# Trace order and conversion pacing in a fused attention and two-layer expert kernel: next gates and first steps before outputs

## The chip, the core and the metric

The kernel runs on one core of a Trainium2 chip. The metric is device time in microseconds for one execution. The core has a matmul engine (TensorE, PE in the rows), a vector engine (VectorE, DVE), a scalar engine (ScalarE, ACT), a general engine (GpSimd, POOL) and a queue engine for transfers (SyncE, SP). Each follows its own list of instructions in order and waits where an input is not there.

## The reference

Windowed attention with four sink columns feeds two dense layers. Shapes: batch 2, 8 heads, 768 tokens, head width 64, so 1536 tokens of 512 channels. All in float32.

```python
x = attn_out.transpose(0, 2, 1, 3).reshape(1536, 512)
g = x @ w_gate                       # 512 x 1536
x = (g / (1 + exp(-g)) * (x @ w_val)) @ w_out      # layer 1, w_out 1536 x 512
h = x @ w_in                         # layer 2, 512 x 2048
out = (max(h, 0) + alpha * min(h, 0)) @ w_out2     # 2048 x 512
```

The weights arrive as 64-bit floats.

## The kernel before

Each product is made of three passes on split operands: high part times high part, low times high, high times low. Weights are split by a conversion, hidden values by `split_hidden` (L691): `hh` on ACT (L692), then `hl` on DVE (L693).

The 1536 tokens are three passes (b = 0, 1, 2) of 512. Layer 1 has a first chunk of four weight columns of 128 (`Moe1.unit`), then four units of two columns (`Duo1.unit`, c = 0 to 3). Units 0 and 3 are plain (`Duo1.plain`, L971): per pass two gate projections (12 matmuls of 512 columns each), two value projections, four outputs of 6 matmuls. Units 1 and 2, and units 1 to 7 of layer 2 (`Duo2.unit`, L1069; unit 0 is plain), treat passes 0 and 1 with a Strassen chain (`Chain.step`, L880): nine steps in `ORDER7`, seven of them products of 6 matmuls into PSUM tiles `pa`, `pb`, `pc`, two full projections of pass 2. Between them ACT copies `pa` to `u1` or `u2` (`keep`, L854), and the next product into `pa` waits for that copy. Twelve outputs follow the chain.

Strassen needs sums. Sums of activations are DVE subtractions and splits, a list `later` of which one is taken per traced step: 14 for layer 1 (`Duo1.sums`, L926), 7 for layer 2 (`Duo2.sums`, L1034), the latter after pass 1 of the last plain unit has its result (`put_y`, L1150). Sums of weights are two items (SUMS, kinds 2 and 3) after each pair of weights that a chain uses; POOL makes them (L567 to L570) and casts them to a high half (L573).

`Stream` feeds the weights. A conversion goes through three calls: `start` (L536, ACT takes the magnitude, L549), `bits` (DVE L584, L587, L590 assemble float32, then ACT's high half `wh`, L593; for sums POOL as above) and `low` (L596, POOL's low half `wl`, L599). `step` (L602) runs each where it can, once per traced step (`tick`, L610). The scratch `w_m` of `start` has two buffers, so a `start` waits until the low half or the sums two items back have read theirs. Converted weights lie in 10 slots (12 at times), given back by `done`.

Trace order is priority: a planner lays out each engine's list before the run, taking of the instructions that are ready by its own times the one traced first. `g.soon()` raises the hidden values. Within `fast` (L1135) `run` (L1219) goes through the units after attention, unit by unit; `verdict` (L363) checks input ranges once the last weight is converted, and ends in a transpose on TensorE and a flag.

Of the kernel before, what the change touches and what calls it, by code (L numbers as in the profile page):

```python
# [11 lines left out]
AF = mybir.ActivationFunctionType  # L12
# [27 lines left out]
VB = 6  # L40
LAG = 2
SOON = 400
ORDER = ((0, 3), (1, 2), (4, 5))
EARLY = 4
WARM = 9
# [317 lines left out]
def verdict(nc, g):  # L363
    scratch = g.t_p.tile([P, T], F32, tag="hid", name="scratch")
    ok, okw = scratch[:, 0:B * H * NQ], scratch[:, B * H * NQ:B * H * NQ + NW]
    nc.vector.tensor_scalar(out=ok, in0=g.nb, scalar1=9.0e8, scalar2=None, op0=ALU.is_lt)
    red = g.red
    nc.vector.tensor_scalar(out=okw, in0=g.wsum, scalar1=WLIM, scalar2=None, op0=ALU.is_lt)
    nc.vector.tensor_reduce(out=red[:, 4:5], in_=okw, axis=AX.X, op=ALU.min)
    nc.vector.tensor_reduce(out=red[:, 0:1], in_=ok, axis=AX.X, op=ALU.min)  # L370
    one = g.const.tile([P, 1], F32, name="one")
    nc.vector.tensor_reduce(out=one, in_=red, axis=AX.X, op=ALU.min)
    ps = g.ps_t.tile([P, 512], F32, tag="ps", name="ps_flag")
    nc.tensor.transpose(ps[:1, :P], one, g.ident)
    fl = g.const.tile([1, 2], F32, name="flag_f")
    nc.vector.tensor_reduce(out=fl[:, 0:1], in_=ps[:1, :P], axis=AX.X, op=ALU.min)
    nc.vector.tensor_scalar(out=fl[:, 1:2], in0=fl[:, 0:1], scalar1=-1.0, scalar2=1.0, op0=ALU.mult, op1=ALU.add)
    g.flag = g.const.tile([1, 1], I32, name="flag")
    nc.vector.tensor_copy(g.flag, fl[:, 1:2])
# [122 lines left out]
class Stream:  # L502
    def __init__(self, nc, g, seq):
        self.nc, self.g, self.seq = nc, g, seq
        self.n_load = self.n_start = self.n_conv = self.n_done = 0
        self.begun = self.halves = None
        self.idle_pool = False
        self.raw, self.w, self.home, self.full = {}, {}, {}, {}
        self.own = range(0)

    def homes(self):

# [39 lines left out]
    def bits(self):  # L552
        nc, g = self.nc, self.g
        (i, rv, m), self.begun = self.begun, None
        kind, src, f, scale, slot = self.seq[i]
        home = self.homes()[0]
        home[1] -= 1
        self.home[i] = home
        wh = home[0].tile([P, KD * P], F32R, tag="wh", name="wh")
        wl = home[0].tile([P, KD * P], F32R, tag="wl", name="wl")  # L560
        self.n_conv += 1
        if kind > 1:
            h = KD * P // 2
            a = self.full[i - kind]
            if kind == 2:
                b, m = self.full[i - 1], self.spare[:, 0:KD * P]
                nc.gpsimd.tensor_tensor(out=m[:, 0:h], in0=b[:, 0:h], in1=b[:, h:], op=ALU.add)  # L567
                nc.gpsimd.tensor_tensor(out=m[:, h:], in0=m[:, 0:h], in1=a[:, 0:h], op=ALU.subtract)
                nc.gpsimd.tensor_tensor(out=a[:, 0:h], in0=a[:, 0:h], in1=b[:, 0:h], op=ALU.subtract)
                nc.gpsimd.tensor_tensor(out=a[:, h:], in0=a[:, h:], in1=m[:, h:], op=ALU.subtract)  # L570
            else:
                m = a
            nc.gpsimd.tensor_copy(wh, m)  # L573
            self.halves = (i, m, wh, wl)
            return
        self.full[i], self.spare = m, rv.rearrange("p c t -> p (c t)").bitcast(F32)
        lo, hi = rv[:, :, 0], rv[:, :, 1]
        mi, mu = m.bitcast(I32), m.bitcast(U32)
        if slot is None or g.exact:
            nc.vector.tensor_scalar(out=m, in0=m, scalar1=WMAX, scalar2=-WMAX, op0=ALU.min, op1=ALU.max)  # L580
            sign, wi = mi, hi
        else:
            sign, wi = hi, mi
        nc.vector.tensor_scalar(  # L584
            out=wi, in0=mi, scalar1=3, scalar2=0x7FFFFFF8, op0=ALU.logical_shift_left, op1=ALU.bitwise_and
        )
        nc.vector.scalar_tensor_tensor(  # L587
            out=mi, in0=sign, scalar=-(2**31), in1=wi, op0=ALU.bitwise_and, op1=ALU.bitwise_or
        )
        nc.vector.scalar_tensor_tensor(  # L590
            out=mu, in0=lo.bitcast(U32), scalar=29, in1=mu, op0=ALU.logical_shift_right, op1=ALU.bitwise_or
        )
        nc.scalar.activation(wh, m, AF.Copy)  # L593
        self.halves = (i, m, wh, wl)
# [5 lines left out]
        self.w[i] = (wh, wl)  # L600

    def step(self):  # L602
        if self.halves:
            self.low()
        if self.begun and self.room():
            self.bits()
        if not self.begun and self.n_load > self.n_start:
            self.start()

    def tick(self, ahead=RB):  # L610
# [85 lines left out]
class Moe1:  # L696
# [4 lines left out]
    def unit(self, c, b):  # L701
# [10 lines left out]
        for x in range(0, CHUNK, 2):  # L712
            pair = hidden_pair(g)
            pss, sgs = [], []
            for r in range(2):
                ps = g.ps_m.tile([P, 512], F32, tag="ps", name="pg")
                proj(nc, ps, st.get(item(0, x + r)), xh, xl)
                pss.append(ps)
                if r == 0:
                    yield  # L720
            for ps in pss:
                sg = g.t_p.tile([P, T], F32, tag="sg", name="sg")
                nc.scalar.activation(sg, ps, AF.Silu)
                sgs.append(sg)
            yield
            for r in range(2):
                hh, hl = (t[:, r] for t in pair)
                ps = g.ps_m.tile([P, 512], F32, tag="ps", name="pv")
                proj(nc, ps, st.get(item(1, x + r)), xh, xl)
                hid = g.t_p.tile([P, T], F32, tag="hid", name="hid")  # L730
                nc.vector.tensor_tensor(out=hid, in0=ps, in1=sgs[r], op=ALU.mult)
                split_hidden(nc, hid, hh, hl)
                hid_of.append((hh, hl))
                if last and r == 1:
                    st.done(4)
                yield
        if c == 0:
            self.accs[b] = new_acc(g, "acc1")
        acc, home = self.accs[b]
# [181 lines left out]
class Duo1(Duo):  # L921
# [48 lines left out]

    def plain(self, w, last):  # L971

        pairs = {}
        _, gate, _, value = self.sinks(pairs)
        for b in range(NPASS):
            pairs[b] = hidden_pair(self.g)
            for i, sink in ((0, gate), (DUO, value)):
                for r in range(DUO):
                    ps = self.new("ph")
                    proj(self.nc, ps, self.st.get(w + i + r), *self.xs[b])  # L980
                    sink(b, r, ps, False)
                    if b == NPASS - 1 and r:
                        self.st.done(DUO)
                    yield
            y = [big(self.g, n) for n in ("yh", "yl")] if last else None
            for m in range(KD):
                self.output(b, m, w + 2 * DUO, *pairs[b], y)
                yield
            if last:
                self.accs[b][1][1] += 1  # L990
                self.put(y, self.accs[b][0])
        self.st.done(DUO)

    def unit(self, c):
# [7 lines left out]
        for i, room, sink in ((0, room_g, gate), (2 * DUO, room_v, value)):  # L1002
            chain = self.chain(w + i, self.ops, self.xs[2], room, sink)
            yield from chain.steps(ORDER7)
            chain.done()
        for b in (2, 0, 1):
            for m in range(KD):
                self.output(b, m, w + 4 * DUO, *pairs[b])
# [19 lines left out]
class Duo2(Duo):  # L1028
# [40 lines left out]
    def unit(self, c, ys):  # L1069
# [9 lines left out]
        else:  # L1079
# [8 lines left out]
                    self.last()  # L1088
            st.done(DUO)
            w += DUO  # L1090
        for b in (2, 0, 1) if c else range(NPASS):
            yield from self.outputs(c, b, w, *pairs[b])
        st.done(DUO)
# [41 lines left out]
def fast(nc, tc, ctx, g, lim, alpha, qk, vp, vs, w_gate, w_val, w_out, x2_in, x2_out, out):  # L1135
# [77 lines left out]
    add_pool(nc, tc, ctx, g.acc_ps, "acc_p2", 1)  # L1213
    for nm, bufs in (("x_p2", 6), ("u_p", 1), ("h_p2", 1), ("t_p2", 4)):
        setattr(g, nm, ctx.enter_context(tc.tile_pool(name=nm, bufs=bufs)))
    st.idle_pool = True
    asked = False

    def run(units):  # L1219
        nonlocal asked  # L1220
        for u in units:
            for _ in u:
                if later:
                    later.pop(0)()
                st.tick()
                if not asked and st.n_conv == len(st.seq):
                    verdict(nc, g)
                    asked = True

    later.extend(d1.sums())  # L1230
    run([m1.unit(0, 2)])
    assert g.w_ps.pop()[1] == WA
    early.close()
    last = (NF1 - CHUNK) // DUO - 1
    with ExitStack() as inner:
        g.x_p3 = inner.enter_context(tc.tile_pool(name="x_p3", bufs=2, side="right"))
        run([d1.unit(c) for c in range(last)])
        assert not later
    add_pool(nc, tc, ctx, g.w_ps, "w_p3", WA, "right")
    st.own = range(base - 3 * DUO, len(st.seq))  # L1240
    run([d1.unit(last)] + [d2.unit(c, ys) for c in range(NF2 // DUO)])
    assert asked and not later


def general(nc, tc, g, q, k, v, w_gate, w_val, w_out, x2_in, x2_out, out):
# [95 lines left out]
```

## Time and profile before

| | |
|---|---|
| median of three runs | 673.70 us (673.52 to 673.95) |
| profiled execution | 673.82 us |
| its span, first to last instruction | 672.1 us |
| TensorE busy | 645.8 us (96%) |
| VectorE busy | 473.8 us (71%) |
| ScalarE busy | 308.7 us (46%) |
| GpSimd busy | 243.5 us (36%) |
| mean granted TensorE clock | 0.985 |

Times of rows are from the span's start. A group row gives busy time, mean duration, then the idle time of the engine before its instructions and what ended it. A wait row gives total, times and longest.

### The profile page before, as it was taken

The numbers are of one execution on the slowest core, as the hardware profiler recorded it, in microseconds if no ns is written. First come the engines' busy times: TensorE is split into PE (matmuls) and PEld (weight loads), VectorE is DVE, ScalarE is ACT, GpSimd is POOL, SyncE is SP. The second block draws the span as 40 slices with busy tenths as digits, with TensorE's granted clock in tenths as the row PEclk, the third lists the DMA queues.
The fourth block names the chain that finished last, engine by engine and source line by source line (L and its number), as shares of the span: only waits on it lengthen the run. The fifth ranks groups of instructions, "written<-read, shape, count | busy, mean of one in ns | idle before, by whom it ended". The sixth has DMA issues, their size and how long they took to land.

```text
span 672.1 us, 8796 instructions
## 1 busy us (share of the span) xinstructions
PE 645.8 (96%) x3032; PEld 506.1 (75%) x3032; DVE 473.8 (71%) x933; ACT 308.7 (46%) x716; POOL 243.5 (36%) x281
## 2 busy tenths in 40 slices
PE   7789899999999899999999989999999999999996
PEld 3457566767788788888878877888888888887885
DVE  6997877353399636678688579848796969686554
ACT  4767856765265214433643335654434252523040
POOL 3547554334113614571334032425344243430000
PEclk8979899999999999999999998999999999999998
DMA  9854444100004203103232111122121213100005
GB/s 273 261 154 144 147 148 134 32 13 1 1 0 130 91 1 93 64 33 126 94 125 95 33 31 62 55 72 63 63 63 63 88 38 95 32 1 0 1 1 192
DMA packets 37205, 52.30 MB, mean 78 GB/s; under 512 B 4385, under 2 KB 28961, under 8 KB 37153
## 3 DMA queue, kind: packets, MB, share of 16 engines
q1 hardware_dynamic: 34944, 51.65, 24.2%
q8 instruction: 26, 0.43, 0.3%
q10 hardware_dynamic: 2208, 0.01, 0.2%
q14 instruction: 27, 0.21, 0.1%
HBM read 48.51 MB, written 3.15 MB: 77 GB/s over the span
## 4 chain that ended last, share of the span: by engine, by line
PE 86%; DVE 5%; ACT 4%; POOL 2%; issue 1%; DMA 1%; SPq 0%; POOLq 0%; ACTq 0%
PE pa L847 9%; PE pf L1105 7%; PE pf L1107 7%; PE pf L1106 7%; PE ph L679 6%; PE ph L680 6%; PE ph L681 6%; PE pb L847 4%; PE po L1018 3%; PE po L1019 3%; PE po L1020 3%; PE xp L321 3%; PE ps_s L225 2%; PE pc L847 2%; PE po L748 2%; PE pg L679 2%
## 5 line engine op out<-in xcount | busy, mean ns | idle before, releaser
L599 POOL TENSOR_TENSOR wl<-w_m,wh 128x512 fp32r<-128x512 f32 x79 | 110.6, 1405 | 197.5 <-ACT wh L593 176.5
L692 ACT ACTIVATE hh<-hid 128x512 fp32r<-128x512 f32 x84 | 52.8, 631 | 83.4 <-DVE hid L966 37.5
L593 ACT ACTIVATE wh<-w_m 128x512 fp32r<-128x512 f32 x68 | 42.9, 631 | 99.3 <-PE pf L1107 40.7
L693 DVE TENSOR_TENSOR hl<-hid,hh 128x512 fp32r<-128x512 f32 x84 | 72.0, 864 | 19.3 <-ACT hh L692 19.2
L1105 PE MATMUL pf<-wh,hh 128*128 128x512 f32 x192 | 75.3, 392 | 0.0
L1106 PE MATMUL pf<-wl,hh 128*128 128x512 f32 x192 | 75.2, 392 | 0.0
L1107 PE MATMUL pf<-wh,hl 128*128 128x512 f32 x192 | 64.7, 392 | 0.0
L584 DVE TENSOR_SCALAR w_m<-w_m 128x512 int32<-128x512 int32 x68 | 35.2, 517 | 37.8 <-ACT w_m L549 37.8
L1112 DVE TENSOR_TENSOR acc<-pf,acc 128x512 f32<-128x512 f32 x84 | 53.3, 683 | 9.8 <-PE pf L1107 9.6
L549 ACT ACTIVATE w_m<-w_raw 128x512 f32<-128x512 f32 x68 | 45.6, 670 | 22.3 <-POOL wl L599 16.6
L587 DVE SCALAR_TENSOR_TENSOR w_m<-w_raw,w_m 128x512 int32<-128x512 int32 x68 | 52.9, 778 | 1.2
L590 DVE SCALAR_TENSOR_TENSOR w_m<-w_raw,w_m 128x512 uint32<-128x512 uint32 x68 | 50.7, 745 | 1.1
L680 PE MATMUL ph<-xl,wh 128*128 128x512 f32 x128 | 49.8, 389 | 0.0
L681 PE MATMUL ph<-xh,wl 128*128 128x512 f32 x128 | 49.8, 389 | 0.0
L679 PE MATMUL ph<-xh,wh 128*128 128x512 f32 x128 | 49.8, 389 | 0.0
L235 ACT ACTIVATE pr<-ps_s,nb 128x160 f32<-128x160 f32 (+2 forms) x96 | 38.0, 406 | 19.5 <-DVE nb L231 17.0
L225 PE MATMUL ps_s<-th 64*128 64x288 f32 (+2 forms) x192 | 39.2, 443 | 7.7 <-ACT pr L235 6.5
L1107 PEld LDWEIGHTS pf<-wh,hl 128*128 128x128 f32 x192 | 36.0, 188 | 8.1
L1018 PE MATMUL po<-hh,wh 128*128 128x512 f32 x96 | 37.8, 394 | 4.5 <-ACT hh L692 4.5
L1106 PEld LDWEIGHTS pf<-wl,hh 128*128 128x128 f32 x192 | 36.0, 188 | 8.1
L1105 PEld LDWEIGHTS pf<-wh,hh 128*128 128x128 f32 x192 | 36.0, 188 | 8.0
L1023 DVE TENSOR_TENSOR acc<-po,acc 128x512 f32<-128x512 f32 x48 | 30.2, 684 | 13.0 <-PE po L1020 13.0
(212 smaller groups left out, 1517.2 us busy)
## 6 DMA issues: line engine op xcount, KB each, us to landing
w_raw<-in_moe_w_out SPq DMA_DIRECT2D x28, 512.0 KB, 3.3
w_raw<-in_moe_w_in SPq DMA_DIRECT2D x16, 512.0 KB, 3.7
w_raw<-in_moe_w_gate SPq DMA_DIRECT2D x12, 512.0 KB, 4.4
w_raw<-in_moe_w_val SPq DMA_DIRECT2D x12, 512.0 KB, 3.6
th<-in_qk SPq DMA_DIRECT2D x16, 336.0 KB, 3.3
vr<-in_v SPq DMA_DIRECT2D x16, 192.0 KB, 2.7
out<-acc SPq DMA_DIRECT2D x12, 256.0 KB, 2.4
th<-in_qk SPq DMA_DIRECT2D x8, 256.0 KB, 5.3
```

The source lines that it names most:

```text
L587: nc.vector.scalar_tensor_tensor(out=mi, in0=sign, scalar=-(2**31), in1=wi, op0=ALU.bitwise_and, op1=ALU.bitwise_or)
L599: eng.tensor_tensor(out=wl, in0=m, in1=wh, op=ALU.subtract)
L679: nc.tensor.matmul(ps, wh[:, c], chan(xh, kk), start=(kk == 0), stop=False)
L680: nc.tensor.matmul(ps, wh[:, c], chan(xl, kk), start=False, stop=False)
L681: nc.tensor.matmul(ps, wl[:, c], chan(xh, kk), start=False, stop=(kk == KD - 1))
L693: nc.vector.tensor_tensor(out=hl, in0=hid, in1=hh, op=ALU.subtract)
L847: self.nc.tensor.matmul(ps, a[:, c], m[:, k], start=(start and k == 0 and y == 0), stop=(k == 1 and y == 2), skip_group_check=True)
L1018: nc.tensor.matmul(ps, wh[:, mc], hh[:, x], start=(x == 0), stop=False)
L1105: nc.tensor.matmul(ps, hh[:, x, ts], wh, start=(x == 0), stop=False)
L1106: nc.tensor.matmul(ps, hh[:, x, ts], wl, start=False, stop=False)
L1107: nc.tensor.matmul(ps, hl[:, x, ts], wh, start=False, stop=(x == DUO - 1))
L1112: nc.vector.tensor_tensor(out=av, in0=ps, in1=av, op=ALU.add)
```

## The change

After `Moe1`'s last pass and in every unit of the two layers, the generator yields a mark, OUT, before its last outputs. The loop in `fast` stops a unit there, traces the first step of the next unit, then the held outputs, then the rest of the next unit. In plain units the gates of pass b + 1 are traced before the outputs of pass b. `Stream.step` does not begin a conversion in a step in which it issued a low half, once `spaced` is set (after attention). The high half of weight sums is an ACT copy in place of a POOL cast. The 14 sums of layer 1 come every second step. The flag's transpose is split from `verdict` into `decide` and traced in the eighth step after the last conversion (LATE).

```diff
+OUT = "outputs"
+LATE = 8
@@ verdict
     nc.vector.tensor_reduce(out=one, in_=red, axis=AX.X, op=ALU.min)
+    g.one = one
+
+
+def decide(nc, g):
     ps = g.ps_t.tile([P, 512], F32, tag="ps", name="ps_flag")
-    nc.tensor.transpose(ps[:1, :P], one, g.ident)
+    nc.tensor.transpose(ps[:1, :P], g.one, g.ident)
@@ Stream.bits
-            nc.gpsimd.tensor_copy(wh, m)
+            nc.scalar.activation(wh, m, AF.Copy)
             self.halves = (i, m, wh, wl)
@@ Stream.step
+        waits = self.spaced and self.halves
         if self.halves:
             self.low()
         if self.begun and self.room():
             self.bits()
-        if not self.begun and self.n_load > self.n_start:
+        if not waits and not self.begun and self.n_load > self.n_start:
             self.start()
@@ Moe1.unit
+        if last:
+            yield OUT
         if c == 0:
             self.accs[b] = new_acc(g, "acc1")
@@ Duo1.plain
-        for b in range(NPASS):
-            pairs[b] = hidden_pair(self.g)
-            for i, sink in ((0, gate), (DUO, value)):
-                for r in range(DUO):
-                    ps = self.new("ph")
-                    proj(self.nc, ps, self.st.get(w + i + r), *self.xs[b])
-                    sink(b, r, ps, False)
-                    if b == NPASS - 1 and r:
-                        self.st.done(DUO)
-                    yield
+        def first(b, i, sink):
+            if i:
+                pairs[b] = hidden_pair(self.g)
+            for r in range(DUO):
+                ps = self.new("ph")
+                proj(self.nc, ps, self.st.get(w + i + r), *self.xs[b])
+                sink(b, r, ps, False)
+                if b == NPASS - 1 and r:
+                    self.st.done(DUO)
+                yield
+
+        def second(b):
             y = [big(self.g, n) for n in ("yh", "yl")] if last else None
             for m in range(KD):
                 self.output(b, m, w + 2 * DUO, *pairs[b], y)
...
+        yield from first(0, 0, gate)
+        for b in range(NPASS):
+            if b < NPASS - 1:
+                yield from first(b, DUO, value)
+                yield from first(b + 1, 0, gate)
+                yield from second(b)
+        yield from first(b, DUO, value)
+        yield OUT
+        yield from second(b)
         self.st.done(DUO)
@@ Duo1.unit, Duo2.unit: before the outputs
+        yield OUT
@@ fast
-    st.idle_pool = True
+    st.idle_pool = st.spaced = True
+    asked = 0
+    def step():
...
+        if later:
+            x = later.pop(0)
+            if x:
+                x()
+        st.tick()
+        if st.n_conv == len(st.seq):
+            asked += 1
+            if asked == 1:
+                verdict(nc, g)
+            elif asked == LATE:
+                decide(nc, g)
...
-    later.extend(d1.sums())
+    later.extend(x for y in d1.sums() for x in (None, y))
...
+    for u, then in units + [(d2.unit(c, ys), None) for c in range(NF2 // DUO)]:
+        for x in u:
+            if x is OUT:
+                break
+            step()
+            if held:
+                for _ in held[0]:
+                    step()
+                if held[1]:
+                    held[1]()
+                held = None
+        held = u, then
+    for _ in u:
+        step()
```

## Rows read from the trace of the kernel before

**Rows 1.** The page's first section: busy us, share of the span, instructions

```profile
PE 645.8 (96%) x3032; PEld 506.1 (75%) x3032; DVE 473.8 (71%) x933; ACT 308.7 (46%) x716; POOL 243.5 (36%) x281
```

**Rows 2.** Stretches: length, busy PE, PEld, DVE, ACT, POOL, granted clock, DMA share, GB/s

```profile
180.00:672.10 492.10, 480.45 (x2098) 393.62 (x2096) 358.52 (x522) 195.78 (x366) 160.80 (x144) 0.99 0.19 62
226.00:230.00 4.00, 4.00 (x18) 3.31 (x19) 3.80 (x4) 0.13 (x1) 2.08 (x2) 1.00 0.10 19
...
405.45:408.85 3.40, 3.40 (x10) 2.59 (x8) 3.40 (x6) 1.71 (x3) 0.00 (x0) 0.51 0.00 0
...
390.00:430.00 40.00, 37.46 (x158) 30.36 (x157) 36.47 (x48) 22.63 (x39) 14.22 (x12) 0.96 0.12 40
```

**Rows 3.** TensorE's waits from 180 us on: total us, times, longest

```profile
PE po L1018 <- ACT hh L692: 4.5, 2, 2.5
PE pa L847 <- ACT u L857: 1.1, 2, 0.7
```

**Rows 4.** Timeline of TensorE: start, duration, instruction, idle before it and its releaser

```profile
226.00 0.50 PE L1018 MATMUL po<-hh,wh 128*128 128x512 f32 x1 [1.99 <-ACT hh L692]
...
403.99 0.50 PE L1018 MATMUL po<-hh,wh 128*128 128x512 f32 x1 [2.54 <-ACT hh L692]
...
665.73 0.39 PE L1107 MATMUL pf<-wh,hl 128*128 128x512 f32 x1
```

**Rows 5.** Timeline of TensorE, first and last of nine starts at the lower clock

```profile
405.48 0.58 PE L1018 MATMUL po<-hh,wh 128*128 128x512 f32 x1
...
408.85 0.44 PE L679 MATMUL ph<-yh,wh 128*128 128x512 f32 x1
```

**Rows 6.** Timeline of TensorE at full clock, first and fifteenth start, between two Strassen steps

```profile
452.04 0.39 PE L680 MATMUL ph<-yl,wh 128*128 128x512 f32 x1
...
455.22 0.39 PE L847 MATMUL pa<-yh,wh 128*128 128x512 f32 x1
```

**Rows 7.** Chain of waits before 226 us: start, duration, engine, tile, line

```profile
222.41 0.74 POOL w_m L569
...
223.18 0.76 ACT w_m L549 x2
...
223.97 0.04 DVE w_m L584
...
224.60 0.69 DVE hid L966
```

**Rows 8.** Chain of waits before 404 us

```profile
393.86 1.13 DVE acc L833
...
399.84 2.23 DVE acc L833
...
402.68 0.61 DVE hid L966
```

**Rows 9.** Timeline: POOL's first low half for layer 1's units; first output matmul

```profile
189.16 1.29 POOL L599 TENSOR_TENSOR wl<-w_m,wh 128x512 fp32r<-128x512 f32 x1 [15.35 <-ACT wh L593]
...
202.09 0.39 PE L748 MATMUL po<-hh,wh 128*128 128x512 f32 x1
```

**Rows 10.** ACT's waits for POOL from 180 us on: total us, times, longest

```profile
ACT w_m L549 <- POOL wl L599: 14.0, 18, 1.4
...
ACT w_m L549 <- POOL w_m L569: 5.3, 3, 3.0
```

**Rows 11.** Groups from 180 us on: busy us, mean ns, idle before and releasers

```profile
L593 ACT ACTIVATE wh<-w_m 128x512 fp32r<-128x512 f32 x56 | 35.3, 630 | 90.8 <-PE pf L1107 40.7 <-DVE w_m L590 19.3 <-PE pa L847 12.2
L857 ACT ACTIVATE u<-pa 128x512 f32<-128x512 f32 x33 | 19.5, 592 | 38.5 <-PE pa L847 38.5
...
L573 POOL CAST wh<-w_raw 128x512 fp32r<-128x512 f32 x11 | 9.6, 876 | 48.2 <-PE ph L680 28.0 <-PE pa L847 20.1
...
L567 POOL TENSOR_TENSOR w_raw<-w_m 128x256 f32<-128x256 f32 x11 | 8.5, 773 | 36.9 <-PE pa L847 26.5 <-issue 8.6 <-DVE w_m L590 1.9
L573 POOL CAST wh<-w_m 128x512 fp32r<-128x512 f32 x11 | 7.6, 691 | 7.4 <-PE ph L680 5.0 <-PE pb L847 2.3
```

More of the change, by code (lines that the diff above doesn't have):

```diff
@@ L509, in __init__ @@
         self.own = range(0)
+        self.spaced = False
     def homes(self):
@@ L971, in plain @@
     def plain(self, w, last):
-        pairs = {}
+        pairs, ys = {}, {}
         _, gate, _, value = self.sinks(pairs)
-        for b in range(NPASS):
-            pairs[b] = hidden_pair(self.g)
-            for i, sink in ((0, gate), (DUO, value)):
-                for r in range(DUO):
-                    ps = self.new("ph")
-                    proj(self.nc, ps, self.st.get(w + i + r), *self.xs[b])
-                    sink(b, r, ps, False)
-                    if b == NPASS - 1 and r:
-                        self.st.done(DUO)
-                    yield
+        def first(b, i, sink):
[9 more added lines that the diff above has]
+        def second(b):
             y = [big(self.g, n) for n in ("yh", "yl")] if last else None
@@ L1090, in unit @@
             w += DUO
+        yield OUT
         for b in (2, 0, 1) if c else range(NPASS):
@@ L1215, in fast, with lend, back @@
         setattr(g, nm, ctx.enter_context(tc.tile_pool(name=nm, bufs=bufs)))
-    st.idle_pool = True
-    asked = False
-    def run(units):
+    st.idle_pool = st.spaced = True
+    asked = 0
+    def step():
         nonlocal asked
[L1221 to L1228, printed above, removed]
-    later.extend(d1.sums())
-    run([m1.unit(0, 2)])
-    assert g.w_ps.pop()[1] == WA
-    early.close()
+        if later:
[9 more added lines that the diff above has]
+                decide(nc, g)
+    inner = ExitStack()
     last = (NF1 - CHUNK) // DUO - 1
-    with ExitStack() as inner:
+    def lend():
+        assert g.w_ps.pop()[1] == WA
+        early.close()
         g.x_p3 = inner.enter_context(tc.tile_pool(name="x_p3", bufs=2, side="right"))
-        run([d1.unit(c) for c in range(last)])
+    def back():
         assert not later
[L1239 to L1242, printed above, removed]
+        inner.close()
+        add_pool(nc, tc, ctx, g.w_ps, "w_p3", WA, "right")
+        st.own = range(base - 3 * DUO, len(st.seq))
+    later.extend(x for y in d1.sums() for x in (None, y))
+    units = [(m1.unit(0, 2), lend)] + [(d1.unit(c), back if c == last - 1 else None) for c in range(last + 1)]
+    held = None
[9 more added lines that the diff above has]
+                    held[1]()
+                held = None
+        held = u, then
+    for _ in u:
+        step()
+    assert asked >= LATE and not later
 def general(nc, tc, g, q, k, v, w_gate, w_val, w_out, x2_in, x2_out, out):
```

## The prediction

> **What bounds the kernel now.** The page's first section gives TensorE 645.8 us of a 672.1 us span [rows 1], so the first question is not which engine is busiest but where TensorE is not busy. A table by stretch divides the missing 26.3 us. From 180 us to the end TensorE lacks 492.1 - 480.45 = 11.65 us [rows 2]; the other 14.65 lie before, in the attention stage. The diff changes nothing that is traced before 180 us: `spaced` is set after attention, and the first two passes of `Moe1.unit` yield no OUT. So those stay. Of the 11.65 us, 672.1 - 666.12 = 5.98 lie after the last matmul [rows 4] (eviction and last output transfers) and stay too. What is left is 5.67 us, and the list of TensorE's waits after 180 us names all of it: 4.5 us in two waits of output matmuls for `hh`, 1.1 us in two waits of a Strassen step for `u` [rows 3].
>
> The reader should next look at the two large waits as events. At 226.00 the outputs of plain unit 0 (third pass) start after 1.99 us of idling, at 403.99 those of the last plain unit after 2.54 us [rows 4]. [...] Between the matmuls starting at 405.48 and 408.85 there are eight steps, 3.37 us [rows 5]; at full clock 14 steps take 455.22 - 452.04 = 3.18 us [rows 6], 0.227 each, so eight take 1.82 and the slow stretch cost 1.55 us.
>
> Last, the chain of waits says why `hh` was late. At 226 it leaves TensorE: the POOL sums up to L569, then ACT's `w_m` L549, which could not start before L569 had read its scratch, then DVE's L584 for that `w_m`, and only behind that, in DVE's queue, the `hid` that TensorE needs [rows 7]. A weight conversion that nobody needs yet holds up the hidden values. At 404 the chain is DVE alone: accumulator additions, `yl` splits and the sums for the next layer, one after the other until 402.68, then `hid`, then `hh` [rows 8]. One 128x1024 sum takes 1.13 us there and a later one 2.23.
>
> **The change part by part.**
>
> *Gates and first steps traced ahead of outputs.* The matmuls are the same 3032; only their order moves, so nothing is added. In a plain unit 24 matmuls (two gates of the next pass, 24 x 0.227 = 5.4 us) now lie between the last value and the outputs. At a unit's end it is one step: 6 matmuls (1.36 us) of Strassen step 1, or 12 (2.72 us) of a full projection. How much this covers: `hh` for r = 0 can start when the value projection r = 0 ends, and the projection r = 1 (12 matmuls, 2.72 us) covered it so far. At 226 `hh` was therefore 2.72 + 1.99 = 4.71 us behind; the new cover is 2.72 + 1.36 = 4.08, so order alone leaves 0.6 us of the stall. At 404 it was 2.72 + 2.54 = 5.26 behind; the new cover is 5.44, so order alone hides it.
>
> The price at 404: the outputs of pass 1 now stand after the gates of pass 2, so from their end to the outputs of pass 2 there are three projections (8.2 us) where there were four (10.9 us), and DVE must do its evictions and splits inside that. Against it, the summing steps are taken one per traced step, and only three steps, not four, now come before those outputs; each is worth 1.13 to 2.23 us of DVE [rows 8]. Bounds for what is left of the 404 stall: none, or all of it with its clock, 2.54 + 1.55 = 4.09. I take none, since one fewer sum and 2.7 us less of window nearly balance and the extra projection is on top. [...]
>
> *Conversions two steps behind.* `start` no longer follows `bits` in the step in which a low half is still pending. From the counters in the code, 2 conversions now start in 4 steps where 4 did; a Strassen unit of layer 1 needs 10 in 30 steps, one of layer 2 needs 6 in 21, so the rate suffices. Counting step by step, the shortest lead from a weight's low half to its first use falls from 7 steps to 4 (first gate of plain unit 0, also because its use moves ahead of four outputs); the first gates of the following units keep 8. In time: that first low half was done at 189.16 + 1.29 = 190.45, and the outputs ahead of which its use now goes started at 202.09 [rows 9], a lead of 11.6 us for a conversion that the change may shift by a step or two (2.7 to 5.4 us). No cost. The loads on SP's queue are issued by the same count of unconverted weights, later by those steps at most; no output transfer is queued there before the last unit. What it removes: ACT's 18 waits for `wl` (14.0 us) and 3 for the sums (5.3 us) [rows 10]. Only one of these, the 3.0 us one, reached TensorE: it is the head of the chain at 226. So the 0.6 us that order leaves there goes as well; bounds 0 to 0.6, I take 0.
>
> *The sums' high half moves from POOL to ACT.* 22 casts of 0.876 or 0.691 us leave POOL, 17.2 us in all; 22 x 0.63 = 13.9 us come to ACT [rows 11], which is busy 195.78 of 492.1 us after 180 [rows 2]. The work itself is hidden. But it adds a wait: the copy on ACT now waits for POOL's two to four half-size sums, about 4 x 0.773 = 3.1 us together at the mean of the first [rows 11], and behind it on ACT stand `u`, `neg`, `sg` and `hh`, for which TensorE waits. The nearest rows for a wait of ACT for POOL's sums are the three of 1.8 us on average, the longest 3.0 [rows 10]. The nearest margin: between step 6 and step 7 of a Strassen chain TensorE has 14 other matmuls, 3.18 us [rows 6], and `u` itself takes 0.59 [rows 11], so 2.6 us of delay are free. Bounds per pair: 0 (or a trifle below, since POOL's relief shortens what DVE and ACT wait for), up to 3.0 + 2 x 0.63 - 2.6 = 1.7 us; for 11 pairs 0 to 18 us. I take 0, because the mean of 1.8 with one copy of 0.63 stays inside 2.6.
>
> [...]
>
> *The rest.* `decide` puts the flag's transpose (one short matmul) eight steps after its input; TensorE did not wait for it before, so no gain, and 0.3 us of work moves. The 14 sums of layer 1 come every second step, 28 of the 36 steps that lie before the first Strassen unit, so they end in time; TensorE has no wait there [rows 3], so no gain either.
>
> **The sum.** The profiled execution took 673.82 us, 672.1 of it span. 673.82 - 1.99 - 2.54 - 1.55 = 667.74. The two small waits (1.1 us) I leave in: they are a matter of which steps happen to adjoin. The median of the three runs is 673.70, 0.12 lower, which changes nothing. Prediction 667.7; if the small ones go too, 666.6.
>
> **Rivals.**
> *The handover stays late.* DVE's queue before the 404 outputs is as late as its window is shorter, and the stall with its slow clock stays in part or whole: 667.74 + up to 4.09, so 668.8 to 671.8, the middle 670.3. For it: DVE is busy 36.47 of the 40 us from 390 [rows 2]. Against: the sums start later.
> *The order was already so.* A planner picks TensorE's order by priority and by its own times; before the change it already pulls matmuls of later projections between outputs. If its times hide the same delays, old stalls go and new ones of like size come: 673.8. For it: both large stalls were delays that its plan did not hold. Against: gates and first steps are ready at once and now stand first.
> *ACT behind POOL (slower).* In the 11 pairs of sums, four in layer 1 and seven in layer 2, ACT's copy waits for POOL and holds `u` or `hh` beyond the 2.6 us margin. At 1 us per pair: 667.7 + 11 = 678.7. It decides from 6.08 / 11 = 0.55 us per pair; the bound of 1.7 would give 686. For it: the added wait is real and in order. Against: the measured mean wait stays inside the margin.
>
> **How the numbers follow.** Chances: forecast 0.51, handover 0.19, order already so 0.13, ACT 0.17. Faster by over 0.2% (under 672.35; 0.2% is about what a measurement here can tell from no change): the first two, 0.70, and a little of the third: 0.71. Within: 0.13. Slower: 0.16. The forecast's own range is 666.4 to 668.8. With the handover rival it holds 0.70, so the range must reach the third: 666.4 to 674.2.
>
> **What would show it.** Right: no TensorE wait above 1 us after 180 us, granted clock 1.00 throughout 390 to 430, TensorE's idle time after 180 (without the tail) about 1.1 us, `po` rows preceded by a gate or first step, L573 on ACT. Wrong: waits of TensorE for `u` in units with sums, with ACT's copy waiting for POOL just ahead (ACT rival); a wait of `po` or of layer 2's first projections for `hh` or `yh` near 404 to 430 with a granted clock near 0.5 (handover); several new stalls elsewhere of the old total (order).

## The result, and the profile after

| | before | after |
|---|---|---|
| median (range) | 673.75 us (673.52 to 673.95, 4 runs) | 667.41 us (665.88 to 667.60, 4 runs) |
| profiled execution, its span | 673.82 us, 672.1 us | 667.32 us, 665.6 us |
| mean granted clock of that execution | 0.985 | 0.983 |

The ratio is 0.9901, 95% interval 0.9884 to 0.9918: 1% less time, clear of noise. The forecast of 667.7 us was met. The terms behind it were not all right, as a second profile of the kernel before showed (experiment e15 below): that they add up to the measured time is in part luck.

First the page's first section of the kernel after; its columns are those of [rows 1]. TensorE has the same 3032 matmuls; 22 instructions went from POOL to ACT.

```profile
PE 646.0 (97%) x3032; PEld 507.5 (76%) x3032; DVE 474.8 (71%) x933; ACT 319.8 (48%) x738; POOL 231.7 (35%) x259
```

Then the table by stretch, after, with the columns of [rows 2].

```profile
0.00:180.00 180.00, 166.98 (x925) 113.66 (x927) 114.19 (x411) 112.44 (x350) 83.17 (x137) 0.94 0.40 122
180.00:665.60 485.60, 479.06 (x2111) 393.85 (x2107) 360.58 (x522) 207.31 (x389) 148.50 (x122) 1.00 0.20 62
...
390.00:430.00 40.00, 40.00 (x177) 32.65 (x176) 36.29 (x50) 24.60 (x44) 14.43 (x11) 1.00 0.16 51
```

From 180 us to the end TensorE now lacks 485.6 - 479.06 = 6.54 us, where it lacked 11.65; nearly all of it is the tail after the last matmul. In the 40 us from 390 it is never idle, though DVE is as busy as before (36.29 against 36.47). TensorE's list of waits from 175 us on, after, has one row left, where [rows 3] has two large waits and two small ones (total us, times, longest):

```profile
PE po L1043 <- ACT hh L701: 0.6, 1, 0.6
```

On the timeline of TensorE, after, the outputs of plain unit 0 still find one hidden half late, while those of the last plain unit follow a projection without a gap; these answer to [rows 4].

```profile
231.77 0.50 PE L1043 MATMUL po<-hh,wh 128*128 128x512 f32 x1 [0.56 <-ACT hh L701]
...
402.55 0.40 PE L690 MATMUL ph<-yh,wl 128*128 128x512 f32 x1
402.79 0.39 PE L1043 MATMUL po<-hh,wh 128*128 128x512 f32 x1
```

The `ph<-yh` just ahead of the outputs at 402.79 belongs to layer 2's first projection, the step that is now traced ahead of them. It covers the delay only just. `hid` is done at about 400.1, but on ACT a conversion that waits 2.25 us for POOL's low half stands before `hh`, and `hh` ends at 402.54, 0.25 us ahead of the matmul that reads it. DVE's and ACT's timeline, after:

```profile
399.45 0.69 DVE L977 TENSOR_TENSOR hid<-ph,sg 128x512 f32<-128x512 f32 x1
...
400.72 0.68 ACT L556 ACTIVATE w_m<-w_raw 128x512 f32<-128x512 f32 x1 [2.25 <-POOL wl L606]
...
401.91 0.63 ACT L701 ACTIVATE hh<-hid 128x512 fp32r<-128x512 f32 x1
```

The chain that ended at 231.77, after (start, duration, engine, tile, line), beside [rows 7]:

```profile
223.41 0.75 POOL w_m L576
...
224.18 0.78 ACT w_m L556 x2
...
224.98 1.41 DVE w_m L591
...
226.41 1.66 DVE w_m L594
228.07 0.61 DVE hid L977
...
230.37 0.69 DVE hid L977
231.09 0.64 ACT hh L701
...
231.77 0.50 PE po L1043
```

It is the chain of before, nearly line for line: POOL's sums, ACT's `w_m`, DVE's conversion, and behind them `hid`. The change did not dissolve it. It gave TensorE 24 matmuls of the next gates (5.4 us) to do meanwhile, and only the second of the two hidden halves is still 0.56 us late.

ACT waits for POOL more than before, not less; its list of waits from 180 us on, after, beside [rows 10]:

```profile
ACT w_m L556 <- POOL wl L606: 21.4, 26, 2.2
...
ACT w_m L556 <- POOL w_m L576: 9.4, 9, 1.6
ACT wh L580 <- POOL w_raw L575: 1.1, 1, 1.1
```

The last row is the wait that the change adds, of ACT's copy for POOL's sums: once, 1.1 us. And the copies themselves, after (groups, columns as [rows 11]), are the 22 at 630 ns that were counted:

```profile
L580 ACT ACTIVATE wh<-w_m 128x512 fp32r<-128x512 f32 x11 | 6.9, 630 | 4.7 <-PE ph L689 3.0 <-PE pb L858 1.7
...
L580 ACT ACTIVATE wh<-w_raw 128x512 fp32r<-128x512 f32 x11 | 6.9, 630 | 12.3 <-PE ph L689 8.2 <-PE pa L858 3.0 <-POOL w_raw L575 1.1
```

### The profile page after: what moved, and what is told of

Same layout as the page of the kernel before. It is cut to its first block, busy times and chain, and to the rows that moved or that the text cites. A ratio compares the mean times of both kernels' runs of the same rounds, so it can differ in the third digit from the quotient of the medians.

```text
span 665.6 us, 8776 instructions
## 1 busy us (share of the span) xinstructions
PE 646.0 (97%) x3032; PEld 507.5 (76%) x3032; DVE 474.8 (71%) x933; ACT 319.8 (48%) x738; POOL 231.7 (35%) x259
## 4 chain that ended last, share of the span: by engine, by line
PE 81%; DVE 8%; ACT 4%; issue 2%; POOL 2%; DMA 1%; SPq 0%; ACTq 0%; POOLq 0%; DVEq 0%
PE pa L858 9%; PE pf L1133 7%; PE pf L1132 7%; PE pf L1131 7%; PE ph L688 6%; PE ph L690 6%; PE ph L689 6%; PE pb L858 4%; PE po L1043 3%; PE po L1044 3%; PE po L1045 3%; PE ps_s L227 3%; PE xp L323 2%; PE pc L858 2%; PE ps_p L282 2%
## 5 line engine op out<-in xcount | busy, mean ns | idle before, releaser
L606 POOL TENSOR_TENSOR wl<-w_m,wh 128x512 fp32r<-128x512 f32 x79 | 112.5, 1428 | 231.0 <-ACT wh L600 216.9
L701 ACT ACTIVATE hh<-hid 128x512 fp32r<-128x512 f32 x84 | 52.6, 630 | 72.5 <-DVE hid L977 29.7
L702 DVE TENSOR_TENSOR hl<-hid,hh 128x512 fp32r<-128x512 f32 x84 | 65.0, 778 | 16.9 <-ACT hh L701 16.5
L1133 PE MATMUL pf<-wh,hl 128*128 128x512 f32 x192 | 68.9, 392 | 0.0
L597 DVE SCALAR_TENSOR_TENSOR w_m<-w_raw,w_m 128x512 uint32<-128x512 uint32 x68 | 58.6, 861 | 1.1
L591 DVE TENSOR_SCALAR w_m<-w_m 128x512 int32<-128x512 int32 x68 | 36.7, 539 | 16.0 <-ACT w_m L556 15.4
L1048 DVE TENSOR_TENSOR acc<-po,acc 128x512 f32<-128x512 f32 x48 | 31.8, 686 | 19.4 <-PE po L1045 19.3
L1043 PE MATMUL po<-hh,wh 128*128 128x512 f32 x96 | 37.5, 391 | 0.6 <-ACT hh L701 0.6
```

The source lines that it names most:

```text
L597: nc.vector.scalar_tensor_tensor(out=mu, in0=lo.bitcast(U32), scalar=29, in1=mu, op0=ALU.logical_shift_right, op1=ALU.bitwise_or)
L606: eng.tensor_tensor(out=wl, in0=m, in1=wh, op=ALU.subtract)
L702: nc.vector.tensor_tensor(out=hl, in0=hid, in1=hh, op=ALU.subtract)
L1043: nc.tensor.matmul(ps, wh[:, mc], hh[:, x], start=(x == 0), stop=False)
L1133: nc.tensor.matmul(ps, hl[:, x, ts], wh, start=False, stop=(x == DUO - 1))
```

## The experiments

Theory after the result: the order of the traced steps carries the gain, by giving TensorE work while DVE is late; the spacing and the ACT copy do nothing. Rivals: the spacing shortens the chain at 226; ACT behind POOL costs something; one of the two moves (gates, or first steps of the next unit) suffices. Line numbers differ between the kernels: the output matmul L1018 of before is L1042, L1043 or L1045 elsewhere, and `hh`'s L692 is L701 or L704.

**e1, the order alone.** From the kernel after:

```diff
-            nc.scalar.activation(wh, m, AF.Copy)
+            nc.gpsimd.tensor_copy(wh, m)
...
-    st.idle_pool = st.spaced = True
+    st.idle_pool = True
...
-    later.extend(x for y in d1.sums() for x in (None, y))
+    later.extend(d1.sums())
...
-LATE = 8
+LATE = 1
```

> The kernel before with the trace order alone changed: gates ahead in plain units and each unit's last outputs held until the next unit's first step; weight sums cast on POOL, conversions, sums and the flag's transpose as before. Theory (order carries the gain): 667.7 us, 666.8 to 668.6, both long stalls of TensorE near 226 and 404 us gone or under 1 us, granted clock 1.00 from 390 to 430. Rival (the copy on ACT carries part of it): 669 to 672, one of the long stalls back.

Measured: 667.47 us (667.09 to 667.69), ratio 0.9904, interval 0.9888 to 0.9921, in effect the ratio of the whole change. TensorE's waits after 182 us, e1:

```profile
PE po L1043 <- ACT hh L701: 0.2, 1, 0.2
```

The order carries the whole gain, the two small waits for `u` included.

**e2, the spacing alone.** On the kernel before: `st.idle_pool = st.spaced = True` and the changed condition in `step`.

> Before, with the spacing of the conversions alone: a conversion is traced only in a step in which no low half is pending; the order of units, the POOL cast and the sums are as before. Theory: each engine's list of instructions is the same with and without it, since the planner places by its own times, so the time is that of before (673.6, ratio 1.000), both stalls stay (2.0 and 2.5 us), and ACT waits for POOL's low halves as often (18 times, 14 us). Rival, the step of the prediction: the pacing takes away the waits of ACT for POOL and with them the stall at 226 us: 671.7 or less, ratio 0.997.

Measured: 673.70 us (10 runs), ratio 0.9981, interval 0.9959 to 1.0003. Both stalls stay, and ACT waits for POOL as before; e2, waits of TensorE and of ACT:

```profile
PE po L1042 <- ACT hh L701: 4.5, 2, 2.5
PE pa L858 <- ACT u L868: 1.1, 2, 0.7
```
```profile
ACT w_m L556 <- POOL wl L606: 14.8, 18, 1.6
ACT w_m L556 <- POOL w_m L576: 5.5, 3, 3.0
```

The planner had placed the conversions where it now places them: in the traces of e2 and e15 every engine's instructions stand in the same order, with and without the condition.

**e4, the change without the spacing**, the same from the other side:

```diff
-    st.idle_pool = st.spaced = True
+    st.idle_pool = True
```

> The changed kernel with conversions begun as before (spaced never set). Its lists of instructions on every engine come out the same as the changed kernel's, line for line, as the kernel before with spacing alone has the lists of the kernel before. Theory (pacing by trace order moves nothing, because the planner takes any instruction that is ready when an engine is free): 667.4 us, 666 to 668, one wait of TensorE of about 0.6 us near 232 us. Rival (my prediction's step: pacing removes the POOL and ACT head of the chain at 226): 0.6 us slower or more, a longer wait there.

Measured: 667.37 us (666.34 to 667.46), ratio 0.9898, interval 0.9864 to 0.9933; TensorE's one wait after 182 us is 0.6 us, as after. The spacing is no part of the result.

**e5 and e6, the two moves alone.** e5 has the next pass's gates ahead of the outputs and ignores OUT; e6 holds a unit's last outputs back behind the next unit's first step and leaves the passes as they were. Their core:

```diff
 # e5
+                yield from first(b, DUO, value)
+                yield from first(b + 1, 0, gate)
+                yield from second(b)
...
+            if x is OUT:
+                continue
```
```diff
 # e6
+            yield from first(b, 0, gate)
+            if b < NPASS - 1:
+                yield from first(b, DUO, value)
+                yield from second(b)
...
+            if x is OUT:
+                break
```

> The kernel before with the gates of pass b+1 ahead of the outputs of pass b in plain units, no holding at a unit's end, all else as before. Theory: both long stalls stand before the last outputs of a plain unit, where this puts nothing ahead, so they stay: 673.7 us, 672.4 to 675. If the second one grows because the outputs of pass 1 come one projection pair later, up to 677. Rival (what the gates do upstream changes when DVE is free): one stall gone, 671.8 or 669.7.

> The kernel before with each unit's last outputs held until the next unit's first step, no gates ahead inside plain units, all else as before. Theory: this is the part that covers both long stalls, 0.6 us left at 226 and none at 404: 667.7 to 668.6 us. Rival (gates ahead are needed too): 670 to 673.7, a stall over 1 us left at 226 or 404.

Measured: e5 673.50 us (672.72 to 673.75), ratio 0.9989, interval 0.9980 to 0.9999; e6 671.09 us (670.89 to 671.73), ratio 0.9964, interval 0.9950 to 0.9979. Timeline of TensorE, e5, then e6:

```profile
231.82 0.50 PE L1043 MATMUL po<-hh,wh 128*128 128x512 f32 x1 [0.48 <-ACT hh L701]
...
403.66 0.50 PE L1043 MATMUL po<-hh,wh 128*128 128x512 f32 x1 [2.41 <-ACT hh L701]
```
```profile
228.15 0.50 PE L1042 MATMUL po<-hh,wh 128*128 128x512 f32 x1 [2.95 <-ACT hh L701]
...
419.92 0.50 PE L688 MATMUL ph<-yh,wh 128*128 128x512 f32 x1 [0.76 <-ACT yh L701]
```

Both expectations missed: e5 was to keep both stalls, e6 to cover both. Each move covers one of the two: the gates that at 226, the hold that at 404, while at 226 it leaves a stall of 2.95 us, larger than before, and at layer 2's start a wait of 0.76 us for `yh`. The small waits for `u` (1.1 us in 2) are gone in e6 and stay in e5. In e5 the shorter stall at 226 should have brought 1.5 us, and the median moved by 0.1. The table by stretch of e5 has the reason in its profiled execution, a granted clock of 0.79 behind the stall at 404:

```profile
403.00:411.00 8.00, 7.34 (x25) 5.91 (x26) 8.00 (x11) 4.41 (x9) 1.28 (x1) 0.79 0.20 66
```

From the starts of its matmuls this costs 1.6 us, about what the gates had gained. e5's mean clock is 0.981 in seven of its ten runs, as in the profiled one, where before has 0.983 to 0.984 in most. So most runs of e5 probably lose as much to the clock, but where they lose it only a profile could show. The two moves alone bring 0.1 and 2.5 us, together 6.1 (e1).

**e15, the kernel before once more.** No edit.

> The kernel before once more, as a run of its own, for one question: in its one profile the attention stage ended at 180.0 us, in the profiles of the changed kernel and of every variant at 180.7 to 181.3, although no instruction that starts before 180 us was changed. If that is chance between executions, this profile ends attention at about 181 as well, with granted clock 0.94 over the first 180 us, and the time is 673.6 as always. If something of the edits reaches back into attention, this profile ends it at 180.0 again, with 0.96. The stalls after 180 us are the same two in either case: 2.0 and 2.5 us of idling, and the slow stretch behind the second.

Measured: 673.72 us (10 runs), ratio 1.0006, interval 0.9988 to 1.0024. Table by stretch, e15, and TensorE's timeline:

```profile
0.00:180.00 180.00, 166.24 (x923) 113.46 (x923) 113.95 (x411) 112.32 (x349) 82.53 (x137) 0.93 0.39 122
...
390.00:430.00 40.00, 37.46 (x165) 30.55 (x164) 35.73 (x47) 22.42 (x39) 15.32 (x12) 1.00 0.13 40
```
```profile
227.46 0.50 PE L1018 MATMUL po<-hh,wh 128*128 128x512 f32 x1 [2.01 <-ACT hh L692]
...
405.48 0.50 PE L1018 MATMUL po<-hh,wh 128*128 128x512 f32 x1 [2.54 <-ACT hh L692]
```

The expectation was right on attention and wrong on the slow stretch. The span of e15 is 672.0 us, as that of the profile ahead of the prediction (672.1). But the first gate behind attention starts at 181.46 here and at 180.02 there, with a clock of 0.93 over the first 180 us (0.96 there); and behind the same stall of 2.54 us the clock is 1.00 here, where [rows 2] has 0.51. The two differences nearly cancel: attention ends 1.44 us later, and the slow stretch costs 1.59 us against the same matmuls here. So the later end of attention in the profile after (first gate at 181.11) lies between two executions of one kernel and need not be an effect of the change, and the slow stretch behind the stall is not a fixed part of the time before. e2's profile is of the same kind as e15's.

**e3, the ACT copy alone.** On the kernel before:

```diff
-            nc.gpsimd.tensor_copy(wh, m)
+            nc.scalar.activation(wh, m, AF.Copy)
```

> The kernel before with the weight sums' high half copied on ACT instead of POOL, nothing else. Theory (the copy is hidden work): 673.7 us within 0.2%, TensorE still stalls about 2.0 and 2.5 us near 226 and 404. Rival that it costs (ACT waits for POOL ahead of u and hh): from 675 up, by 1 us in each of 11 pairs 684. Rival that it helps (relief of POOL): under 672.4.

Measured: 675.22 us (673.95 to 675.85, 10 runs), ratio 1.0024, interval 1.0014 to 1.0033. TensorE's waits after 182 us and its timeline, e3:

```profile
PE po L1042 <- ACT hh L701: 5.0, 2, 2.7
PE pa L858 <- ACT u L868: 1.1, 2, 0.7
```
```profile
227.99 0.50 PE L1042 MATMUL po<-hh,wh 128*128 128x512 f32 x1 [2.70 <-ACT hh L701]
...
405.73 0.50 PE L1042 MATMUL po<-hh,wh 128*128 128x512 f32 x1 [2.31 <-ACT hh L701]
```

The time is the rival's (675 up), by another path than the rival named: the waits for `u` are those of before, so ACT does not hold up the Strassen steps. What grew is the stall at 226 (2.70 for 2.01 in e15), in the chain that was there: DVE's first operation on the late `w_m` takes 1.38 us (L591 at 225.30), beside POOL's low half, where in e15 it takes 0.72 (L584 at 225.43), beside POOL's cast. The profiled execution (674.05 us) shows 0.5 us of idling more than before and no slow clock after 180 us, so it does not show where the rest of the 1.6 us goes. Five of the ten runs have a mean clock of 0.979 to 0.982 and take 675.65 us or more, the others 674.8 or less; of the 20 runs of before beside them five have 0.977 to 0.981. Why the copy alone meets the lower clock more often, or whether that is chance, is open; no profile of such a run exists.

**e7, the change with POOL's cast**, the reverse of e3's edit on the kernel after.

> The changed kernel with the weight sums' high half cast on POOL as before. Theory (with the new order the copy's engine costs and brings nothing): 667.4 us, 666.6 to 668. Rival (alone the copy cost 1.6 us, so here its return to POOL gains as much): 665.8.

Measured: 667.22 us (667.00 to 668.79), ratio 0.9918, interval 0.9893 to 0.9943. TensorE waits 0.2 us once, as in e1; with ACT's copy it waits 0.56 us (after, e4). With the new order the time does not tell which engine makes the high half.

**e9, slower sums on POOL.** On the kernel after, the first two of the four half-size sums are written three times:

```diff
+                for _ in range(2):
+                    nc.gpsimd.tensor_tensor(out=m[:, 0:h], in0=b[:, 0:h], in1=b[:, h:], op=ALU.add)
+                    nc.gpsimd.tensor_tensor(out=m[:, h:], in0=m[:, 0:h], in1=a[:, 0:h], op=ALU.subtract)
```

> The changed kernel with the first two of POOL's four sum instructions of each pair written three times, 4 more POOL instructions of about 0.76 us, 3 us, ahead of ACT's copy in each of 11 pairs. Theory (the copy's wait is hidden, because the list of ACT is laid out with POOL's times): 667.4 us within 0.2%, TensorE's waits after 180 us under 1.5 us in all. Rival (ACT behind POOL): 3 us of delay against a margin of 2.6 us, so from 0.4 us per pair, 672, to 3 us per pair, 700.

Measured: 667.55 us (667.27 to 667.67), ratio 0.9905, interval 0.9871 to 0.9938. ACT's waits after 180 us, one of the two groups of the added operations, and the copy's longest wait and the longest in a Strassen unit, e9:

```profile
ACT w_m L556 <- POOL wl L609: 25.6, 29, 2.3
...
ACT w_m L556 <- POOL w_m L579: 15.7, 8, 3.9
ACT wh L583 <- POOL w_raw L578: 4.7, 3, 3.2
```
```profile
L578 POOL TENSOR_TENSOR w_raw<-w_raw,w_m 128x256 f32<-128x256 f32 x22 | 21.4, 972 | 1.7
```
```profile
227.24 0.63 ACT L583 ACTIVATE wh<-w_raw 128x512 fp32r<-128x512 f32 x1 [3.18 <-POOL w_raw L578]
...
489.02 0.63 ACT L583 ACTIVATE wh<-w_raw 128x512 fp32r<-128x512 f32 x1 [0.78 <-POOL w_raw L578]
```

The dose arrives at ACT: its copy waits 4.7 us in three, up to 3.2, where it waited 1.1 once. It does not arrive at TensorE, which has no wait in its list after 182 us. So the third rival costs nothing even with POOL's sums lengthened. The margin of 2.6 us between Strassen steps was not put to the test by this: the wait of 3.2 us lies in plain unit 0, and in the Strassen units the copy waited 0.78 us, twice.

**e13, the head of the chain taken away.** On the kernel before, POOL's four sums of the first pair of weights are not made (the first layer's result is then another):

```diff
+                if i == next(j for j, s in enumerate(self.seq) if s[0] == 2):
+                    m = b
+                else:
                     nc.gpsimd.tensor_tensor(out=m[:, 0:h], in0=b[:, 0:h], in1=b[:, h:], op=ALU.add)
```

> The kernel before without POOL's four sum instructions of the first pair of weight sums (unit 1's gates; the third and fourth weights are used unsummed, so layer 1's result is not the reference's). Theory (the stall near 226 us comes from POOL's sums, on which ACT's next w_m waits, with DVE's list and hid behind it): stall under 0.5 us there, the one at 404 stays, 671.6 us. Rival (DVE late for its own conversions): stall stays about 2 us, 673.6.

Measured: 672.71 us (670.76 to 673.28, 10 runs), ratio 0.9973, interval 0.9953 to 0.9994. TensorE's waits after 182 us, DVE's timeline, and the stretch at 404, e13:

```profile
PE po L1045 <- ACT hh L704: 2.5, 1, 2.5
PE pa L861 <- ACT u L871: 1.1, 2, 0.7
```
```profile
222.63 0.69 DVE L980 TENSOR_TENSOR hid<-ph,sg 128x512 f32<-128x512 f32 x1 [2.87 <-PE ph L693]
```
```profile
403.00:411.00 8.00, 8.00 (x28) 6.46 (x29) 8.00 (x12) 3.85 (x5) 0.28 (x1) 0.79 0.08 21
```

DVE's timeline in e15, for comparison:

```profile
225.43 0.72 DVE L584 TENSOR_SCALAR w_m<-w_m 128x512 int32<-128x512 int32 x1 [5.44 <-ACT w_m L549]
...
226.07 0.68 DVE L966 TENSOR_TENSOR hid<-ph,sg 128x512 f32<-128x512 f32 x1
```

`hid` now starts as soon as TensorE's projection is there, and the stall at 226 is gone while that at 404 stands. That POOL's sums cause the stall at 226 is thereby shown. The links between are read from the chain [rows 7]: POOL's sums hold ACT's `w_m`, this holds DVE's conversion, and `hid` stands behind it in DVE's queue; in e13 the planner also put `hid` ahead of the conversion. The time does not reach the expected 671.6 us, because in e13's profile, as in e5's, the clock falls behind the stall at 404: 1.6 us, from the starts of the matmuls, against the 2.28 that the stall at 226 costs in e15.

**e10 and e11, a third scratch buffer** for `w_m`, on the kernel before and on the kernel after:

```diff
-        m = g.raw_w.tile([P, KD * P], F32, tag="m", name="w_m")
+        m = g.raw_w.tile([P, KD * P], F32, tag="m", name="w_m", bufs=3)
...
-    g.zero = once.tile([P, T], mybir.dt.bfloat16, name="zero")
+    g.zero = g.vsr[:, 0].bitcast(mybir.dt.bfloat16)
```

> The kernel before with three scratch buffers in place of two for conversions (room made by letting the warm-up operand share the memory of a later value tile), order as before. Theory (the stall near 226 comes from a conversion on ACT that waits for POOL to read the scratch, with DVE's list behind it): that stall goes, the one at 404 stays, 671.5 us, 670.5 to 672.5. Rival (DVE is late there for its own load): stall stays at 2 us, 673.7. The attention stage is planned anew too, so the waits after 180 us decide, not the time alone.

> The changed kernel with three scratch buffers. Theory: the last 0.6 us wait of TensorE near 232 goes, 666.6 us, 665.8 to 667.6, if the attention stage keeps its time. Rival (DVE's own load): it stays, 667.4.

Measured: e10 683.77 us, ratio 1.0147, interval 1.0113 to 1.0182; e11 669.62 us, ratio 0.9934, interval 0.9907 to 0.9962. Timeline of TensorE, e10:

```profile
228.69 0.50 PE L1042 MATMUL po<-hh,wh 128*128 128x512 f32 x1 [2.67 <-ACT hh L701]
...
361.56 0.50 PE L1042 MATMUL po<-hh,wh 128*128 128x512 f32 x1 [2.84 <-ACT hh L701]
```

Both expectations missed: the stall stays, with POOL's sums still at its head, and a new one comes at 361. With a third buffer the planner lays the lists out anew: in e10 all three of DVE's operations on the late `w_m` stand ahead of `hid`, where one does in before. e11 keeps one wait of 0.5 us, now at 234.27, and what it loses against after lies in the attention stage, whose first gate comes at 183.68 where after has 181.11. The pair says nothing on the cause at 226; e13 does. That more scratch does not help is what it shows.

## Why the prediction was right, step by step

The span fell by 672.0 - 665.6 = 6.4 us from e15 to after, whose mean clocks are 0.981 and 0.983 and which have no slow stretch after 180 us. The terms beside the prediction's, with the excess of each stall read from the starts of the matmuls (time from one start to the next, less 0.227 us a matmul):

| term | predicted, us | from e15 to after, us |
|---|---|---|
| stall at 226, idling | -1.99 | -2.01 + 0.56 = -1.45 |
| stall at 404, idling | -2.54 | -2.54 |
| slow clock behind it | -1.55 | 0 |
| two small waits for `u` | 0 (down to -1.1) | -1.14 |
| restart of TensorE after a stall | not counted | -0.84 |
| attention stage | 0 | -0.35 (181.46 to 181.11) |
| sum | -6.08 | -6.3 |

**The bound.** Right: TensorE's stalls after 180 us were all there was to gain, and DVE's chains set them (shown by e13 for the one at 226, read from [rows 8] for the one at 404). Of the signs named, one missed: the idle time left is 0.56 us and not about 1.1, as the small waits went too.

**Order.** Right at 404, for the reason given: e6 alone removes that stall, and in after the cover of 5.44 us leaves 0.25. At 226 the 0.6 us that order was to leave is what is left (0.56), but the working behind it is wrong. The prediction took the event for the third pass at the unit's end, with one first step as cover. 48 matmuls of `ph` start at 212.97 in the trace of before and the outputs follow: these are gates and values of the first pass. So the cover is the next pass's gates (5.4 us), and e5, without any hold, shows 0.48 us there, while the hold alone leaves 2.95. Why this larger cover doesn't hide all: the half that is late now is the second. DVE makes its `hid` at 230.37, where e15 has it at 230.63; in the kernel before, 12 matmuls of the next gates lay between the outputs of the two halves and hid that. They now stand with the other gates ahead of both. The agreement is a coincidence.

**Conversions two steps behind.** Wrong. The step said that the spacing takes away ACT's waits for POOL and with them the last 0.6 us. It moves no instruction (e2, e4), the waits for `wl` grew from 14.0 to 21.4 us (to 21.4 without the spacing too, in e4), and 0.56 us stay. One of these waits, the 2.25 us ahead of `hh` at 404, nearly reached TensorE. The argument counted traced steps; the planner does not follow their order where its own times already say the same.

**The slow clock.** This is the term that was mis-sized. The stretch of 1.55 us was in one execution of the kernel before and not in e15, nor in e2, whose instructions stand in the same order; in e5 and e13 it came again. The sum took it as gone with the idling; that was the author's estimate, and no run shows the term: behind the same 2.54 us of idling the clock was 0.51 in the first profile of before and 1.00 in e15, and from e15 to after the slow clock gives 0. At the clock that most runs have, 0.983 to 0.984 before and 0.982 to 0.983 after, the spans are 671.6 to 672.4 us in the runs of before beside e1, e3, e5 and e6, and 665.6 to 665.9 after: the whole 6 us come with no change of the mean clock.

**The small waits and the restart.** These stood in for that term. The prediction left 1.1 us in, as a matter of adjoining steps; with the hold other matmuls stand between just those (the waits are gone in e1 and e6, there in e3, e5, e13). And each of these stalls cost TensorE more than its idle row: at 226 in e15 the excess is 2.28 us with 2.01 of idling, at 404 2.82 with 2.54, at the two small ones 1.69 with 1.14; after, 0.82 with 0.56. Less after's one, that is 0.27 + 0.28 + 0.55 - 0.26 = 0.84 us. So two gains did not come, the clock's 1.55 and 0.54 at 226, and three came that the sum did not hold, these two (2.0 together) and 0.35 from attention. They happen to match within 0.3 us. That the forecast lies so near is luck in this; the stalls, the larger part of the sum, are not.

**ACT's copy.** It cost nothing that the times show in the change, as taken (e7 against after). The reason, a margin of 2.6 us between Strassen steps, was not needed: the copy waited for POOL once, 1.1 us, in plain unit 0, and in e9 no longer than 0.78 us in a Strassen unit. Alone it costs 0.24% (e3), not through `u`, which was the path that the third rival named. How an instruction that waits holds up one behind it, the trace shows on DVE: in e15 it idles 5.44 us until `w_m` is there and makes `hid` only behind it, at 226.07, though the projection for `hid` ended at 222.7. The 678.7 us of the third rival did not come.

**The rivals.** The handover showed itself only in e6, 0.76 us for `yh`, and not in the kernel after. "The order was already so" holds for the spacing, and in part at 226, where the planner had put 12 matmuls of the next gates between outputs; for the rest of the gates and for the first steps it does not. ACT behind POOL fell: TensorE waits for `u` neither in after nor in e9.

## What to carry to other kernels

Where a value reaches TensorE late through a chain on other engines, it can be enough, as here, to trace other ready matmuls ahead of its use; the chain itself may stay. Each of two such places needs its own filler, and the time of one filler alone need not show what it covers (e5). Before a slow stretch of the clock is entered in a sum, look whether a second execution of the same kernel has it, and compare runs at the same mean clock. An edit of pacing in the source is worth nothing where a planner gives the same instruction lists, so compare these first.

## What the runs showed of the hardware

The length of a stall did not tell whether the granted clock fell behind it. It fell to 0.51 after 2.54 us in the first profile of before (0.79 over 403 to 411 us) and stayed at 1.00 after the same 2.54 us in e15; over 403 to 411 us it was 0.79 in e5, with a stall of 2.41 us, and 0.79 in e13, with one of 2.5; e6 stayed at 1.00 in the 6 us around a stall of 2.95, e3 after 2.70 and 2.31. Tables by stretch, e6 and e3:

```profile
226.00:232.00 6.00, 3.85 (x17) 3.19 (x18) 5.30 (x6) 1.79 (x4) 3.66 (x3) 1.00 0.40 145
```
```profile
226.00:232.00 6.00, 4.01 (x18) 3.32 (x19) 5.93 (x10) 1.93 (x4) 1.80 (x2) 1.00 0.54 176
...
403.00:411.00 8.00, 5.69 (x25) 4.38 (x24) 8.00 (x11) 4.19 (x7) 0.86 (x1) 1.00 0.00 0
```

What decides it stays open, as does where the slow stretches of the first 100 us fall (mean clock there 0.93 in the first profile of before, 0.88 in e15, 0.90 in after). And the five stalls read here, four in e15 and one in after, cost 0.26 to 0.28 us each beyond the idle row: the row of the matmul in front lasts 0.39 us where the next start otherwise comes after 0.227, and from the first one after the stall to the next start it is 0.34 us. Some of DVE's operations on `w_m` took longer beside POOL's work: after 180 us in e15, with POOL at rest, L584 takes 0.41 to 0.43 us and L587 0.67 to 0.69, beside POOL's low half up to 1.54 (at 207.13) and 1.75 (at 300.04), though others beside it took no longer (0.42 at 269.90, 0.69 at 416.62).
